# Where a range check's small VectorE sums stand, and how much ScalarE time a planner counts for one matrix unit

## The chip, the cores and the metric

The kernel runs on one core of one Trainium2 chip. The metric is the device time of one execution in microseconds. Every run's time is that of the whole program on the device; a profiled execution also gives its span, from the first to the last instruction.

## The reference, cut to what is computed

One block of a network on 2048 rows of width 512, all in fp32: two modulated layer norms, a Fourier mixing step written as matrix products with cosine and sine tables, and a gated feed-forward step of inner width 1792.

```python
mod = (_silu(c) @ w_mod).reshape(1, 6, 1, -1)
sa, ca, ga, sb, cb, gb = (mod[:, i] for i in range(6))
h = _layernorm(x) * (1 + ca) + sa
a, b = h @ dft_hid_re.T, h @ dft_hid_im.T
x = x + ga * (dft_seq_re @ a - dft_seq_im @ b)
h = _layernorm(x) * (1 + cb) + sb
x = x + gb * ((_silu(h @ w1) * (h @ w3)) @ w2)
```

(The last seven lines stand for the reference's `einsum` calls, with the same operands.)

## The kernel before

**Numbers as pairs.** TensorE multiplies in fp32r. Each fp32 operand is split into a high part (a copy by ScalarE, rounded to fp32r) and a low part (the difference, by VectorE), and a product takes three passes: high by high, high by low, low by high (`PASSES`). So each operand costs one ScalarE and one VectorE instruction, and the copies and differences named `hf`, `h2h`, `w3h`, `w3l`, `w3sh`, `w3sl` are these.

**Stages.** The kernel first makes the modulation and the first layer norm with the hidden transform, then the transform along the sequence, then the second layer norm, and from about 260 us on the feed-forward part. There the inner width is cut into 7 groups of 256 columns (`NG = 7`), and the rows into 4 tiles of 512, which are taken in two pairs: pair 0 are the tiles 0 and 2, pair 1 the tiles 1 and 3. `items` lists the pieces of work in their order: groups 2 to 6 of pair 0, then groups 0 to 6 of pair 1, twelve in all. `turning` is 5, the number of the first item of pair 1.

**Strassen units.** In one item both first products, with `w1` (kind "a") and with `w3` (kind "b"), are 2x2 block products done with seven multiplications each, in a Strassen form. `factor(i, w, n)` does multiplication n: six matmuls of 128x512 into one PSUM bank, then what reads the bank. For n of 1, 5 and 6 ScalarE copies the bank to a tile `x`; for 2, 3 and 7 VectorE adds an earlier copy to the bank; n = 4 is used as it stands. The bank goes on being accumulated into: multiplication 7 adds to the bank that 6 left, so its first matmul has to wait until ScalarE has copied the bank out. Results of "a" pass through a Silu on ScalarE; results of "b" are multiplied by them on VectorE (`times(v, v, src)`), which gives `v`, the operand of the second product.

**Second products.** The five items of `SEVEN` (groups 0 to 4 of pair 1) also do their second product, with `w2`, in seven multiplications. One of them is a unit of `seven_unit` (line 1325): six matmuls into two banks, two read-outs by ScalarE into a tile `y` (line 335, scaled by `gb`), and one DMA, issued by GpSimd, that adds `y` to a sum in DRAM (line 1352). The other items use `down_unit`: one bank and one read-out a unit; for the last two groups of pair 1 VectorE adds the bank straight to the tile `xr` that will be the output (line 1146).

**Order on the engines.** There is no scheduler here that moves instructions: each engine runs its own instructions in the order in which this Python code writes them, and waits on semaphores. The order of the units is a string written by hand, one for each item. The item before the last, number 10, and the last, number 11, have

```python
if i == len(items) - 2:
    body = "a6 y a5 y a7 a3 y a4 b1 y b2 b6 y b5"
if i == len(items) - 1:
    head = "-b7 y a1 a2 y -b4 y -b3 "
    body = "a6 a5 a7 a3 a4 b1 b2 y b6 y b5 y b7 y b4 y y b3 y y y y y y y y y y"
```

where "a6" is multiplication 6 of kind "a" of this item, "-b4" multiplication 4 of kind "b" of the item before, and "y" one unit of second products. So items overlap: the last three multiplications of "b" stand in the head of the next item.

**What is written between the units.** `behind(n, fn)` keeps a step back until n units later (`delayed()` runs at the start of each unit). In items that are not of `SEVEN` the high part of a `v` comes one unit after it and the low part two units after it. The weights for the coming items are loaded, split and summed by steps in the queue `jobs`. After each unit, `beside(us, used)` says how long the unit takes on TensorE (1.36) and how much of that it uses of VectorE and of ScalarE; the rest is credit, and steps of `jobs` are written as long as the credit of their engine is above zero:

```python
for n, us in enumerate((dve, act)):
    credit[n] = min(credit[n] + us, max(us, 1.0))
...
    if any(us > 0 and credit[n] <= 0 for n, us in enumerate(cost)):
        return
```

`USED["y"]` is (0.0, 0.6): a unit "y" is counted as 0.6 us of ScalarE and leaves it a credit of 0.76.

**The check's sums.** Squares of the transform tables are summed by ScalarE into the tile `chk` early in the kernel. `judge()` (line 1009) makes one number of them, `bad`: a memset of the tile `sq` by GpSimd (line 1014), then 15 small VectorE instructions (lines 1015 to 1035). At the program's very end every engine reads `bad` and branches: if it is set, a general version of the whole computation runs, which it does not for these inputs. `judge()` is called in `unit`, right behind multiplication 4 of kind "b" of the item `turning + 1`, which is item 6, so in the head of item 7.

Of the kernel before, what the change touches and what calls it, by code (L numbers as in the profile page):

```python
# [23 lines left out]
NG = F // (2 * P)  # L24
# [18 lines left out]
def folded(nc, pools, c, cp, wmr, wmc, x, xt, ctr, cti, wdr, wdi, w1, w3, w2, out):  # L43
# [73 lines left out]
    def advance(dve, act=9.0, queue=background):  # L117

        for n, us in enumerate((dve, act)):
            credit[n] = min(credit[n] + us, max(us, 1.0))  # L120
        while queue and len(free) >= queue[0][0] + kept():
            _, *cost, fn = queue[0]
            if any(us > 0 and credit[n] <= 0 for n, us in enumerate(cost)):
                return
            queue.popleft()
            if fn is None:
                return
            for n, us in enumerate(cost):
                credit[n] -= us
            fn()  # L130

    def drain(ready, queue=background):
        while not ready():
            fn = queue.popleft()[-1]
            if fn is not None:
                fn()
# [875 lines left out]
    def judge():  # L1012
        sq = consts.tile([P, 3, 32], F32, name="sq")
        nc.gpsimd.memset(sq, 0.0)
        nc.vector.tensor_reduce(
            out=sq[:, 0, :8],
            in_=chk.rearrange("p a b n -> p (a b) n"),
            axis=AX.X,
            op=OP.add,
        )  # L1020
        nc.vector.transpose(sq[:, 1, :], sq[:, 0, :])
        r = small.tile([P, 1], F32, name="jr", tag="jr")
        nc.vector.tensor_reduce(out=r, in_=sq[:, 1, :], axis=AX.X, op=OP.add)
        for a in range(4):
            nc.vector.tensor_copy(sq[:32, 2, a : a + 1], r[32 * a : 32 * a + 32, :])
        nc.vector.tensor_reduce(out=r[:32], in_=sq[:32, 2, :], axis=AX.X, op=OP.add)
        nc.vector.tensor_copy(sq[:32, 0, :], r[:32].to_broadcast([32, 32]))
        nc.vector.transpose(sq[:32, 1, :], sq[:32, 0, :])
        own = small.tile([1, 4], F32, name="own", tag="jo")
        nc.vector.tensor_scalar(own, sq[0:1, 1, 4:8], SMALL, None, op0=OP.mult)  # L1030
        fine = small.tile([1, 4], F32, name="fine", tag="jf")
        nc.vector.tensor_tensor(out=fine, in0=sq[0:1, 1, 0:4], in1=own, op=OP.is_lt)
        times(fine[:, 0:2], fine[:, 0:2], fine[:, 2:4])
        times(fine[:, 0:1], fine[:, 0:1], fine[:, 1:2])
        nc.vector.tensor_scalar(bad, fine[:, 0:1], -1.0, 1.0, op0=OP.mult, op1=OP.add)
# [42 lines left out]
    def delayed():  # L1078
        for fn in later.pop(1, ()):
            fn()  # L1080
        for n in sorted(later):
            later[n - 1] = later.pop(n)


    def up_block(g, t, q, w):
        if q == 0 and w == "w1":
            drain(lambda: ("h2", t, 1) in done)
        to = bank(turn[0] % 4)
        turn[0] += 1
        for d in range(ND):  # L1090
            at = slice(d * P, (d + 1) * P)
            product(
                to,
                [u[:, q, at] for u in wuse[w, g]],
                [u[t, d // 2][:, d % 2, :] for u in (h2h, h2l)],
                d == 0,
                d == ND - 1,
            )
        if t == PAIRS[0][1] and q == 1:
            give_w((w, g))  # L1100
        if w == "w1":
            cur["v"] = take(F32, "v")
            nc.scalar.activation(cur["v"][:, 0, :], to, AF.Silu)
        else:
            v = cur.pop("v")
            times(v[:, 1, :], v[:, 0, :], to)
            u = hf[g, t, q] = take(F32R, "hf")
            copy(u[:, 0, :], v[:, 1, :])
            behind(1, lambda: minus(u[:, 1, :], v[:, 1, :], u[:, 0, :].bitcast(F32)))
            behind(1, lambda: give(v))  # L1110
# [63 lines left out]
    items = [(g, 0) for g in range(2, NG)] + [(g, 1) for g in range(NG)]  # L1174
# [50 lines left out]
    SEVEN = [(g, 1) for g in range(NG - 2)]  # L1225
# [104 lines left out]
    def seven_unit(g, pair, n, key):  # L1330
        new = n in (1, 2, 5)
        if new:
            banks7[:] = [bank(6), bank(7)]
        y = take(F32, "y")
        which, k = TO7[n]
        t = PAIRS[pair][k]
        names = ("h", "l") if LEFT7[n][0] == "h" else ("sh", "sl")
        u = right7.pop(((g, pair), n))
        for e, to in enumerate(banks7):
            at = int(LEFT7[n][1]) * HALF + e * P  # L1340
            product(
                to,
                [flat(wuse[key][x])[:, at : at + P] for x in names],
                [u[:, b, :] for b in range(2)],
                new,
                True,
                not new,
            )
            d = 2 * which + e
            copy_by(y[:, e, :], to, gb[:, d : d + 1])  # L1350
        give(u)
        nc.gpsimd.dma_start(sums[t, which], y, accum_op=OP.add)  # L1352
        behind(4, lambda: give(y))
        if n == ORDER7[-1]:
            for x in wuse.pop(key).values():
                give(x)
            if g == NG - 3:
                for t in PAIRS[pair]:
                    load_sums(t)
# [319 lines left out]

    USED = {"w1": (0.0, 0.5), "w3": (1.2, 0.5), "y": (0.0, 0.6), "own": (0.7, 0.0)}
    FACTOR = {
        "a": {1: (0.0, 0.5), 2: (0.6, 0.5), 3: (0.6, 0.5), 4: (0.0, 0.5), 5: (0.0, 0.5)},
        "b": {1: (0.0, 0.5), 2: (1.8, 0.5), 3: (1.8, 0.5), 4: (1.2, 0.5), 5: (0.0, 0.5)},
# [4 lines left out]
    def beside(us, used):  # L1690
        advance(us - used[0], us - used[1], jobs)
        if not jobs:
            advance(0.0, 0.0)

    def up(g, t):
        for q in range(2):
            for w in ("w1", "w3"):
                drain(lambda: ((w, g), "l") in done, jobs)
                delayed()
                up_block(g, t, q, w)  # L1700
                beside(2.72, USED[w])

    def down(g, pair, *which):
        key = which[-1]
        drain(lambda: (key, "l") in done, jobs)
        delayed()
        if (g, pair) in SEVEN:
            seven_unit(g, pair, *which)
        else:
            down_unit(g, pair, *which)  # L1710
        beside(1.36, USED["own" if pair == 1 and g >= NG - 2 else "y"])

    for w in ("w1", "w3"):
        load_w((w, 1))
# [21 lines left out]
    turning = len([at for at in items if at[1] == 0])  # L1736
# [11 lines left out]
    def early_w3(i):  # L1748
        return items[i][1] == 1

    def unit(kind, i, n):
        g, pair = items[i]
        more = i + 1 < len(items)
        if n == 1:
            drain(lambda: ("ready", i, "w1" if kind == "a" else "w3") in done, jobs)
        if (kind, i, n) == ("a", 0, 6):
            drain(lambda: ("t", 0, 4) in done)
        if (kind, i, n) == ("a", turning, 1):
            drain(lambda: not background)
        if kind == "a" and i == turning and n in (4, 5, 6, 7):  # L1760
            drain(lambda: ("t", 1, {6: 2, 5: 1, 7: 3, 4: 4}[n]) in done, jobs)
        delayed()
        factor(i, "w1" if kind == "a" else "w3", n)
        if (kind, i, n) == ("b", turning + 1, 4):
            judge()
        if (kind, n) == ("a", 1):
            load_w(("w1", *items[i + 1]) if more else ("w2", g, pair))
        if (kind, n) == ("a", 6):
            load_w(("w2", g, pair))
        if not more and kind == "a" and state[i, "w1"]["n"] == 7:  # L1770
            down_banks[:] = [6, 7, 0, 1, 2]
        if (kind, n) == ("a", 7 if i == turning else 3) and more:
            load_w(("w3", *items[i + 1]))
            weight_jobs(i + 1, "w1")
        if (kind, n) == ("b", 2):
            (seven_jobs if (g, pair) in SEVEN else plain_jobs)(("w2", g, pair))
        if (kind, n) == ("b", 3):
            if i + 2 == turning:
                drain(lambda: ("xc", 3) in done)
                for at in ((1, 0), (1, 1), (3, 1)):  # L1780
                    chunk_parts(background, *at, 3)
                sums_of.append(pair_sums(background, 1))
            if i + 1 == turning:
                other_operands()
            if more and not early_w3(i):
                weight_jobs(i + 1, "w3")
            if (g, pair) in SEVEN:
                seconds.extend((g, pair, n, ("w2", g, pair)) for n in ORDER7)
            else:
                for t in PAIRS[pair]:  # L1790
                    seconds.extend((g, pair, t, d, ("w2", g, pair)) for d in range(ND))
        if (kind, n) == ("b", 6) and more and early_w3(i):
            weight_jobs(i + 1, "w3")
        beside(1.36, FACTOR[kind][n])
# [835 lines left out]
```

## Time and profile before

| | before |
|---|---|
| time, median of 3 runs | 700.3 us (699.35 to 700.66) |
| profiled execution, time | 698.81 us |
| its span | 697.0 us, so 1.81 us lie around it |
| TensorE busy | 677.9 us, 97% of the span |
| VectorE busy | 587.9 us, 84% |
| ScalarE busy | 451.4 us, 65% |
| GpSimd busy | 133.6 us, 19% |
| instructions | 9026 |

In the rows of the timeline the first number is the start in us from the span's start, the second the time it takes in us; PE is TensorE, DVE VectorE, ACT ScalarE, POOL GpSimd. "out<-in" names the tiles, "x2" two like instructions in one row, and a bracket at the end the idle time of the engine before the row and what ended it. Successive matmuls of 128x512 start 0.226 us apart when nothing holds them, though each is shown with 0.39 us.

### The profile page before, as it was taken

The page shows a single profiled execution, that of the slowest core. Times are in us where ns is not written, and L with a number is a line of the kernel's source. Part 1 is how long each engine was busy: PE and PEld are TensorE (multiplying, and loading weights), DVE is VectorE, ACT ScalarE, POOL GpSimd, SP SyncE. Part 2 cuts the span into 40 slices and gives each one's busy share as a digit, 9 for nine tenths or more (in the row PEclk, how much of TensorE's full clock was granted, in tenths as well). Part 3 has the DMA queues.
Part 4 walks back from the last instruction along what each step waited for, and adds up shares of the span by engine and source line. Part 5 has one row for each costly group of instructions (what it writes and reads, how often), then busy time and mean ns, then how long its engine had stood idle before and what let it go on. Part 6 is the DMA issues. An engine that isn't in the chain of part 4 may idle for free.

```text
span 697.0 us, 9026 instructions
## 1 busy us (share of the span) xinstructions
PE 677.9 (97%) x3122; PEld 557.1 (80%) x3122; DVE 587.9 (84%) x945; ACT 451.4 (65%) x751; POOL 133.6 (19%) x156
## 2 busy tenths in 40 slices
PE   7999899999999999999999999999999999999996
PEld 5898778888888888888877788787877888888785
DVE  5999779987999977989987886898899979888373
ACT  4998965455343665664566767677676978777620
POOL 1320253543445000100100001011002221121100
PEclk9999999999999999999999999999999999999999
DMA  8730299787578431363758566456939898999703
GB/s 265 217 122 1 74 329 364 254 291 243 186 287 294 152 140 31 63 119 121 133 114 166 132 151 124 88 94 144 265 87 200 150 221 163 187 212 170 186 39 125
DMA packets 40261, 116.80 MB, mean 168 GB/s; under 512 B 5136, under 2 KB 5392, under 8 KB 40208
## 3 DMA queue, kind: packets, MB, share of 16 engines
q0 software_dynamic: 14512, 50.86, 35.8%
q1 hardware_dynamic: 25264, 63.98, 27.6%
q10 hardware_dynamic: 432, 1.31, 0.6%
q8 instruction: 26, 0.43, 0.3%
q14 instruction: 27, 0.22, 0.1%
HBM read 76.81 MB, written 41.42 MB: 170 GB/s over the span
## 4 chain that ended last, share of the span: by engine, by line
PE 73%; DVE 11%; ACT 8%; issue 3%; DMA 3%; SPq 1%; another core or an unknown queue 1%; POOL 0%; ACTq 0%; POOLq 0%
PE bank L100 45%; PE bank L750 25%; PE bank L559 1%; DMA wmr<-in_wmr 1%; ACT y L335 1%; DMA sum<-y 1%; ACT hf L87 1%; DVE v L96 1%; PE bank L598 1%; DVE xc L96 1%; SPq L231 1%; ACT xc L894 1%; DVE x L93 1%; DVE w3s L90 1%; DVE v L93 1%
## 5 line engine op out<-in xcount | busy, mean ns | idle before, releaser
L100 PE MATMUL bank<-hf,w2h 128*128 128x512 f32 (+1 forms) x352 | 108.8, 390 | 0.5 <-ACT y L335 0.4
L87 ACT ACTIVATE hf<-v 128x512 fp32r<-128x512 f32 x71 | 44.3, 630 | 64.6 <-DVE v L96 53.8
L335 ACT ACTIVATE y<-bank,gb 128x512 f32<-128x512 f32 x118 | 76.5, 682 | 5.2 <-PE bank L100 5.1
L100 PEld LDWEIGHTS bank<-hf,w2h 128*128 128x128 f32 x352 | 65.4, 188 | 16.9 <-ACT y L335 2.2
L1160 POOL DMA_DIRECT2D sum<-y x28 | 24.0, 857 | 245.1 <-ACT y L335 125.1
L100 PE MATMUL bank<-hf,w2l 128*128 128x512 f32 (+1 forms) x176 | 68.1, 387 | 0.0
L90 DVE TENSOR_TENSOR hf<-v,hf 128x512 fp32r<-128x512 f32 x71 | 48.8, 687 | 13.8 <-ACT hf L87 13.8
L1352 POOL DMA_DIRECT2D sum<-y x35 | 29.8, 852 | 129.3 <-ACT y L335 124.9
L750 PE MATMUL bank<-d,us 128*128 128x512 f32 x128 | 49.9, 390 | 1.0 <-DVE ho L93 1.0
L750 PE MATMUL bank<-bh,us 128*128 128x512 f32 x128 | 49.9, 390 | 0.0
L750 PE MATMUL bank<-bh,ul 128*128 128x512 f32 x128 | 49.8, 389 | 0.0
L750 PE MATMUL bank<-d,uh 128*128 128x512 f32 x128 | 49.8, 389 | 0.0
L750 PE MATMUL bank<-l,us 128*128 128x512 f32 x128 | 49.8, 389 | 0.0
L750 PE MATMUL bank<-l,uh 128*128 128x512 f32 x128 | 49.8, 389 | 0.0
L170 POOL DMA_INDIRECT re<-in_ctr,mirror x32 | 37.2, 1162 | 65.6 <-DVE ul L90 38.5
L87 ACT ACTIVATE x<-bank 128x512 f32<-128x512 f32 x72 | 41.5, 591 | 11.9 <-PE bank L100 11.8
L170 POOL DMA_INDIRECT im<-in_cti,mirror x32 | 32.8, 1025 | 36.6 <-PE bank L750 11.6
L100 PEld LDWEIGHTS bank<-hf,w2l 128*128 128x128 f32 x176 | 33.0, 188 | 6.7
L93 DVE TENSOR_TENSOR v<-bank,x 128x512 f32<-128x512 f32 x36 | 24.7, 687 | 15.9 <-PE bank L100 14.8
L1244 ACT ACTIVATE v<-v 128x512 f32<-128x512 f32 x36 | 22.7, 630 | 23.2 <-DVE v L93 22.8
L93 DVE TENSOR_TENSOR x<-bank,x 128x512 f32<-128x512 f32 x36 | 24.6, 685 | 9.4 <-PE bank L100 9.1
L100 PE MATMUL bank<-h2h,w1h 128*128 128x512 f32 x80 | 31.1, 389 | 0.0
(260 smaller groups left out, 1906.3 us busy)
## 6 DMA issues: line engine op xcount, KB each, us to landing
sum<-y POOLq DMA_DIRECT2D x63, 512.0 KB
w<-in_w SPq DMA_DIRECT2D x42, 512.0 KB
re<-in_ctr SPq DMA_DIRECT2D x32, 256.0 KB
im<-in_cti SPq DMA_DIRECT2D x32, 256.0 KB
wmc<-in_wmc SPq DMA_DIRECT2D x8, 512.0 KB
xr<-in_xt SPq DMA_DIRECT2D x8, 512.0 KB
sum<-xr SPq DMA_DIRECT2D x8, 512.0 KB
x<-in_x SPq DMA_DIRECT2D x11, 256.0 KB
```

The source lines that it names most:

```text
L87: nc.scalar.activation(dst, src, AF.Copy, scale=scale)
L90: nc.vector.tensor_tensor(out=dst, in0=a, in1=b, op=OP.subtract)
L93: nc.vector.tensor_tensor(out=dst, in0=a, in1=b, op=OP.add)
L96: nc.vector.tensor_tensor(out=dst, in0=a, in1=b, op=OP.mult)
L100: nc.tensor.matmul(acc, lhs[a], rhs[b], start=first and n == 0, stop=last and n == len(PASSES) - 1, skip_group_check=more,)
L170: nc.gpsimd.indirect_dma_start(dst, None, rows, bass.IndirectOffsetOnAxis(ap=at, axis=0))
L231: queue.dma_start(raw_w[dt][q * 64 : (q + 1) * 64, m, :], w[i][par::2, q])
L335: nc.scalar.activation(dst, src, AF.Identity, scale=by)
L750: nc.tensor.matmul(acc[what, e], lhs, rhs, start=begin and i == 0, stop=(end or (turn and what == "x")) and i == len(terms) - 1, skip_grou ...
L1160: nc.gpsimd.dma_start(sums[t, d // 2], y, accum_op=OP.add)
L1244: behind(k != 0 or q == 0, lambda: nc.scalar.activation(v, src, AF.Silu))
L1352: nc.gpsimd.dma_start(sums[t, which], y, accum_op=OP.add)
```

## The change

Two edits. In the table `USED` a unit of second products in a `SEVEN` item is now counted with 1.3 us of ScalarE, both its read-outs, where it was counted with 0.6. And `judge()` is written behind multiplication 4 of "b" of item `len(items) - 2`, which is item 10 (the last group but one of pair 1), in the head of the last item, where it was written behind that of item 6.

```diff
-    USED = {"w1": (0.0, 0.5), "w3": (1.2, 0.5), "y": (0.0, 0.6), "own": (0.7, 0.0)}
+    USED = {"w1": (0.0, 0.5), "w3": (1.2, 0.5), "y": (0.0, 0.6), "y7": (0.0, 1.3), "own": (0.7, 0.0)}
...
             down_unit(g, pair, *which)
-        beside(1.36, USED["own" if pair == 1 and g >= NG - 2 else "y"])
+        wide = (g, pair) in SEVEN
+        beside(1.36, USED["own" if pair == 1 and g >= NG - 2 else "y7" if wide else "y"])
...
         factor(i, "w1" if kind == "a" else "w3", n)
-        if (kind, i, n) == ("b", turning + 1, 4):
+        if (kind, i, n) == ("b", len(items) - 2, 4):
             judge()
```

TensorE's and SyncE's order stay as they were, instruction for instruction. On ScalarE five pairs of neighbours change places, one in each of the items 6 to 10, and nothing else. In items 6 to 9 it is the high part of the next `w3` (`w3h`) and the copy of bank 5 after multiplication 5 of "b" (`x`): `w3h` stood first and now stands second. In item 10 it is the high part of the sums of `w3` (`w3sh`) and the same copy `x`. ScalarE's rows there, before:

```order
L335 ACTIVATE y_5833<-bank_952_5831,gb 128x512
L335 ACTIVATE y_5833<-bank_953_5832,gb 128x512
L87 ACTIVATE w3sh_5845<-w3s_5825 128x1024
L87 ACTIVATE x_5854<-bank_957_5847 128x512
L87 ACTIVATE hf_5866<-v_5622 128x512
```

And ScalarE's rows of the changed kernel at the same place:

```order
L335 ACTIVATE y_5813<-bank_952_5811,gb 128x512
L335 ACTIVATE y_5813<-bank_953_5812,gb 128x512
L87 ACTIVATE x_5832<-bank_956_5825 128x512
L87 ACTIVATE w3sh_5834<-w3s_5805 128x1024
L87 ACTIVATE hf_5846<-v_5602 128x512
```

What moved is `w3sh`, behind one bank copy; the high part `hf` behind both keeps its place.

On VectorE the 15 instructions of `judge()` leave the head of item 7 and stand in the head of item 11. There VectorE's rows were, before, from the product of multiplication 4 (`v` with `bank`) on:

```order
L96 TENSOR_TENSOR v_5622<-v_5622,bank_943_5782 128x512
L90 TENSOR_TENSOR hf_5918<-v_5622,hf_5918 128x512
L93 TENSOR_TENSOR x_5789<-bank_957_5847,x_5789 128x512
L96 TENSOR_TENSOR v_5621<-v_5621,x_5789 128x512
L90 TENSOR_TENSOR hf_5947<-v_5621,hf_5947 128x512
```

In the changed kernel VectorE has, from inside the sums on (six of their rows, beginning with the tile `sq`, stand between that product and these):

```order
L1028 STREAM_TRANSPOSE sq<-sq 32x32
L1030 TENSOR_SCALAR own<-sq 1x4
L1032 TENSOR_TENSOR fine<-sq,own 1x4
L96 TENSOR_TENSOR fine<-fine 1x2
L96 TENSOR_TENSOR fine<-fine 1x1
L1035 TENSOR_SCALAR bad<-fine 1x1
L90 TENSOR_TENSOR hf_5918<-v_5602,hf_5918 128x512
L93 TENSOR_TENSOR x_5769<-bank_956_5825,x_5769 128x512
L96 TENSOR_TENSOR v_5601<-v_5601,x_5769 128x512
L90 TENSOR_TENSOR hf_5947<-v_5601,hf_5947 128x512
```

The sums now stand ahead of the low part `hf_5918`, of the addition `x` from the bank of multiplication 3, and of the product `v` made from it.

On GpSimd the memset of `sq` goes along. Its last rows, before:

```order
L1352 DMA sum_0_3248<-y_5833 128x1024
L1352 DMA sum_0_3779<-y_5868 128x1024
L1352 DMA sum_1_3781<-y_5901 128x1024
L1352 DMA sum_1_3250<-y_5920 128x1024
L2566 TENSOR_LOAD bad
```

And those of the changed kernel:

```order
L1352 DMA sum_0_3248<-y_5813 128x1024
L1352 DMA sum_0_3779<-y_5848 128x1024
L1352 DMA sum_1_3781<-y_5881 128x1024
L1014 MEMSET sq 128x96
L1352 DMA sum_1_3250<-y_5920 128x1024
L2567 TENSOR_LOAD bad
```

The memset now stands behind the last DMA but one of the second products, where at its old place (behind the DMA of another unit) it is gone.

## The prediction, as it was put on record

> **What bounds the kernel now.** I read the page first, then who TensorE waited for, then the timeline of each engine around the two places of the sums and the five swapped pairs.
>
> The page of the kernel before, its head and the busy times:
>
> ```profile
> span 697.0 us, 9026 instructions
> PE 677.9 (97%) x3122; PEld 557.1 (80%) x3122; DVE 587.9 (84%) x945; ACT 451.4 (65%) x751; POOL 133.6 (19%) x156
> ```
>
> TensorE is busy for 97% of the span, and its order does not change. So the time moves only where TensorE's next matmul starts later or earlier than now. TensorE's waits from 450 to 560 us, which is where the old place of the sums lies:
>
> ```profile
> PE bank L100 <- ACT y L335: 1.0, 2, 0.6
> PE bank L100 <- DVE v L93: 0.3, 1, 0.3
> PE bank L100 <- ACT x L87: 0.2, 1, 0.2
> ```
>
> From 560 us to the end the same view lists no wait. That is not quite so: a matmul is drawn with 0.39 us while the next one starts 0.226 us after it, so a wait shorter than the difference stays hidden. I therefore go by the distances between starts.
>
> **The old place of the sums: what goes.** The timeline of the kernel before, VectorE's and GpSimd's rows, then ScalarE's (the third is from the next item, where no sums stand), then TensorE's:
>
> ```profile
> 532.08 0.68 DVE L96 TENSOR_TENSOR v<-v,bank 128x512 f32<-128x512 f32 x1
> 532.42 0.85 POOL L1352 DMA_DIRECT2D sum<-y  x1 [3.89 <-ACT y L335]
> 532.96 0.51 POOL L1014 MEMSET sq<- 128x96 f32 x1
> 533.50 0.42 DVE L1015 TENSOR_REDUCE sq<-chk 128x8 f32<-128x256 f32 x1 [0.75 <-POOL sq L1014]
> ...
> 536.52 0.67 DVE L90 TENSOR_TENSOR hf<-v,hf 128x512 fp32r<-128x512 f32 x1
> 537.12 0.67 DVE L93 TENSOR_TENSOR x<-bank,x 128x512 f32<-128x512 f32 x1
> ```
>
> ```profile
> 539.28 0.63 ACT L87 ACTIVATE hf<-v 128x512 fp32r<-128x512 f32 x1 [2.57 <-DVE v L90]
> 539.82 1.25 ACT L335 ACTIVATE y<-bank,gb 128x512 f32<-128x512 f32 x2
> ...
> 566.25 0.64 ACT L87 ACTIVATE hf<-v 128x512 fp32r<-128x512 f32 x1 [0.22 <-DVE v L90]
> ```
>
> ```profile
> 539.76 0.39 PE L100 MATMUL bank<-th,w1sl 128*128 128x512 f32 x1
> 540.54 0.72 PE L100 MATMUL bank<-hf,w2h 128*128 128x512 f32 x2 [0.39 <-ACT y L335]
> ```
>
> The sums wait for the memset, which starts 0.54 us after the DMA issue ahead of it (532.42 to 532.96); the first sum starts 0.54 us after that. From the first sum to the low part behind them VectorE needs 3.02 us (533.50 to 536.52). All of it delays the `v` for which ScalarE's `hf` waits 2.57 us; the read-out `y` stands behind that `hf`, and TensorE needs the bank that `y` empties. Its start comes 0.78 us after the one before, 0.55 too late, and its first pair takes 0.72 where a pair takes 0.61: 0.66 us together. One item later, without sums, the same `hf` waits 0.22 us and TensorE not at all. **Gain here: 0.66 us**, at least 0 if another wait steps in at once, at most this.
>
> **The swaps in items 6 to 9: nothing.** ScalarE's rows in the last of the four, then the VectorE row that reads `w3h`:
>
> ```profile
> 610.88 1.06 ACT L87 ACTIVATE w3h<-w 128x1024 fp32r<-128x1024 f32 x1
> 611.83 0.60 ACT L87 ACTIVATE x<-bank 128x512 f32<-128x512 f32 x1
> 612.31 1.28 ACT L335 ACTIVATE y<-bank,gb 128x512 f32<-128x512 f32 x2
> ```
>
> ```profile
> 613.47 1.22 DVE L90 TENSOR_TENSOR w3l<-w,w3h 128x1024 fp32r<-128x1024 f32 x1
> ```
>
> A copy takes 0.48 us of ScalarE's row (611.83 to 612.31). Put first, it starts at 610.88, and `w3h` runs from 611.36 to 612.42; the read-out behind both stays at 612.31. `w3l` comes at 613.47, 1.05 us after that, behind other VectorE work. The copy of bank 5 comes 0.95 us earlier, but what reads it stands behind `w3l` too. The cover is that 1.05 us of VectorE's backlog; were it gone, 0.48 us would be lost an item.
>
> **The swap in item 10: 0.46 us lost.** Here the pair is `w3sh` and the copy. TensorE's last matmul of multiplication 5, then ScalarE, VectorE, and TensorE's next wait:
>
> ```profile
> 639.80 0.39 PE L100 MATMUL bank<-th,w3sl 128*128 128x512 f32 x1
> ...
> 645.24 0.39 PE L100 MATMUL bank<-h2h,w1l 128*128 128x512 f32 x1
> 645.73 0.73 PE L100 MATMUL bank<-hf,w2sh 128*128 128x512 f32 x2
> ```
>
> ```profile
> 640.77 1.07 ACT L87 ACTIVATE w3sh<-w3s 128x1024 fp32r<-128x1024 f32 x1
> 641.72 0.60 ACT L87 ACTIVATE x<-bank 128x512 f32<-128x512 f32 x1
> 644.47 0.63 ACT L87 ACTIVATE hf<-v 128x512 fp32r<-128x512 f32 x1 [2.15 <-DVE v L96]
> 645.01 1.25 ACT L335 ACTIVATE y<-bank,gb 128x512 f32<-128x512 f32 x2
> ```
>
> ```profile
> 641.89 1.22 DVE L90 TENSOR_TENSOR w3sl<-w3s,w3sh 128x1024 fp32r<-128x1024 f32 x1
> ```
>
> The bank is ready at 640.19, so the copy starts at 640.77 without a wait and `w3sh` runs from 641.25 to 642.32. VectorE's `w3sl`, which started 0.05 us after `w3sh` ended, starts at 642.35 and not at 641.89: 0.46 later. VectorE has no slack behind it: the addition and the `v` follow at once, ScalarE's `hf` waits 2.15 us for that `v`, `y` stands behind `hf`, and TensorE's start at 645.73, already 0.26 late, waits for `y`. So all of it is 0.46 us later from here on. Bounds: 0, if VectorE had slack that the rows do not show, and 0.48, the whole copy.
>
> **The new place of the sums: 2.33 us more.** VectorE and GpSimd, ScalarE, and TensorE in the head of item 11:
>
> ```profile
> 648.80 0.69 DVE L96 TENSOR_TENSOR v<-v,bank 128x512 f32<-128x512 f32 x1 [1.33 <-PE bank L100]
> 649.58 0.85 POOL L1352 DMA_DIRECT2D sum<-y  x1 [2.18 <-ACT y L335]
> ...
> 651.81 0.69 DVE L93 TENSOR_TENSOR x<-bank,x 128x512 f32<-128x512 f32 x1 [0.94 <-PE bank L100]
> 652.54 0.69 DVE L96 TENSOR_TENSOR v<-v,x 128x512 f32<-128x512 f32 x1
> ```
>
> ```profile
> 653.40 0.63 ACT L87 ACTIVATE hf<-v 128x512 fp32r<-128x512 f32 x1 [2.10 <-DMA sum<-y]
> 653.94 1.19 ACT L87 ACTIVATE x<-bank 128x512 f32<-128x512 f32 x2
> ```
>
> ```profile
> 654.11 0.39 PE L100 MATMUL bank<-th,w1sl 128*128 128x512 f32 x1
> 654.57 0.50 PE L100 MATMUL bank<-th,w1sh 128*128 128x512 f32 x1
> ```
>
> Unlike at the old place, item 10 is not of `SEVEN`: the high part `hf` of the `v` from multiplication 3 is due one unit later and so stands ahead of ScalarE's copy of bank 0 after multiplication 6, and multiplication 7 (654.57) cannot start before that copy. The sums stand ahead of that `v` on VectorE. Step by step, with the 0.46 us:
>
> - The DMA issue comes at 649.58 + 0.46 = 650.04, the memset 0.54 later at 650.58, the first sum 0.54 later at 651.12. VectorE, free at 649.95, has waited 1.17 us.
> - The low part behind the sums: 651.12 + 3.02 = 654.14. The addition 0.60 later (536.52 to 537.12): 654.74. The `v` 0.73 later (651.81 to 652.54): 655.47, done after 0.69 at 656.16.
> - ScalarE's `hf` at 656.19; the DMA that it waited for now (653.40) has landed long before. The copy 0.54 later (653.40 to 653.94): 656.73. TensorE 0.63 after the copy's start (653.94 to 654.57): 657.36.
>
> That is 2.79 us later than 654.57, of which 0.46 is the swap. TensorE stands still for 2.56 us there (it would be ready at 654.11 + 0.23 + 0.46). Behind it the matmuls already stand end to end, so nothing gives the time back. Bounds for the sums here: below, as if they began as soon as VectorE is free (651.12 - 1.15), which takes 1.15 off; above, 2.79 alone with no gain elsewhere.
>
> What is queued behind the sums on VectorE has been named; behind the waiting `hf` on ScalarE stand both copies, for multiplications 7 and 3. GpSimd has one DMA behind the memset, and no one waits for it before VectorE's first addition to the output tiles, in the first "y" of the last item's body, seven multiplications on.
>
> **A stall that long and TensorE's clock.** The start of the trace has one of like length; TensorE's row and the stretch behind it (the value behind the busy times of the five engines is the granted clock):
>
> ```profile
> 9.00 1.10 PE L485 MATMUL bank<-ident,x 128*128 128x128 f32 x4 [2.08 <-DVE x L470]
> ...
> 10.00:15.00 5.00, 5.00 (x29) 3.87 (x28) 4.26 (x7) 2.69 (x5) 0.00 (x0) 0.76 1.08 274
> ```
>
> After 2.08 us of idleness five microseconds went at 0.76 of the clock, 1.2 us of work lost. If the new stall did the same, the loss would be 2.79 + 1.2. The row is from a TensorE that had just begun, and I take nothing for it, but keep it as a rival. The Trainium skill, "TensorE: Matmul & The Clock Gate", section "HAM oscillation — how this bites in real kernels", says that only idle gaps of more than about 3.4 us bring the half clock back; by it the sum has no such term, as the stall is an estimated 0.8 us short of that. No run here has yet shown a gap of this length in a warm TensorE.
>
> **The sum.** -0.66 + 0.46 + 2.33 = +2.13 us. The profiled execution took 698.81 us, 697.0 of span and 1.81 around it; with the change 700.94. That execution lies 1.49 us under the median of the runs, 700.3; on the median's footing the changed kernel takes 702.4 us, 0.3% longer.
>
> **Rivals.**
>
> 1. *VectorE's idle time in the last item takes the sums in.* VectorE waits 1.33 and 0.94 us for TensorE around the new place, so little work might seem free there. Then only the old stall goes: 700.3 - 0.66 = 699.6. Against it: TensorE loses nothing only if the copy starts by 654.17, so the sums would have to begin by 648.56, before the product ahead of them is even made (648.80). Chance 0.06. If the swaps freed TensorE from all 1.5 us that the waits from 450 to 560 list, it would be 698.8, faster than before; but the waits for `y` and `x` there stand on instructions that are not moved. Chance 0.03.
> 2. *The memset runs at once.* If GpSimd did not hold it behind the DMA issue, or the issue came early, the sums would begin at 649.97: +2.13 - 1.15 = +0.98, 701.3. Against it stands the old place, where VectorE waited 0.75 us for that memset. Chance 0.10.
> 3. *The old stall does not go.* If another ScalarE wait holds `y` at 540 us, the gain is lost: 700.3 + 2.79 = 703.1. For it: ScalarE is full there. Against it: the next items have the same order and no wait. Chance 0.09.
> 4. *The stall costs clock as well:* 702.4 + 1.2 = 703.6. Chance 0.06.
>
> **How the numbers follow.** My forecast has 0.66, with the swap in item 10 between 0 and 0.48, so 702.0 to 702.4 before the scatter of the runs (1.3 us from lowest to highest). About 0.2%, 1.4 us, is what a measurement of this kernel can tell from no change, so the line lies at 701.7. Rivals 3 and 4 and nearly all of the forecast lie above it, 0.77; rivals 1 and 2 mostly below, with a rest of the forecast, 0.19; faster 0.04. The range goes from 701.1, which takes in rival 2, to 703.6, rival 4.
>
> **What would show it.** In the changed kernel's trace: no late start of TensorE near 540 us; `w3l` of items 6 to 9 with no wait for `w3h`; `w3sl` near 642 about 0.46 us later against TensorE; the sums starting about 0.54 us after the memset, 3.0 us long, in the head of item 11; and one start of TensorE some 2.8 us after the one before it, with ScalarE's copy `x` behind an `hf` that waited for VectorE's `v`. I am wrong if TensorE goes through multiplication 7 of the last item without that gap, or if it gains more than 0.7 us before 640 us.

## The result and the profile after

Six runs of the changed kernel have a median of 705.22 us (704.39 to 707.65), six of the kernel before, measured beside it, 699.83 (698.79 to 700.66). Slower, by 5.4 us between the medians. The ratio on record, which is not that of the medians, is 1.0084, with a 95% interval of 1.0070 to 1.0099. The prediction had 702.4 with a range up to 703.6. Its side was right, its size was not.

The profiled execution of the changed kernel took 705.42 us, 6.61 more than that of before. The head of its page:

```profile
span 703.6 us, 9020 instructions
...
PE 679.8 (97%) x3122; PEld 558.9 (79%) x3122; DVE 588.2 (84%) x945; ACT 451.9 (64%) x751; POOL 132.5 (19%) x156
```

TensorE has the same 3122 matmuls, and is busy 1.9 us longer with them (677.9 before). The whole program has 9020 instructions and not 9026, although the change takes no work away: by the records of the traces, VectorE has five waiting instructions fewer and SyncE one (352 records before, 351 after). Both are traces of what the prediction lacked. First what it had, in the order of its steps. TensorE's timeline at the old place, then ScalarE's in item 9 and VectorE's row behind it:

```profile
540.50 0.39 PE L100 MATMUL bank<-th,w1sl 128*128 128x512 f32 x1
540.73 0.61 PE L100 MATMUL bank<-hf,w2h 128*128 128x512 f32 x2
```

```profile
610.39 1.08 ACT L87 ACTIVATE x<-bank 128x512 f32<-128x512 f32 x2
611.35 1.07 ACT L87 ACTIVATE w3h<-w 128x1024 fp32r<-128x1024 f32 x1
612.30 1.27 ACT L335 ACTIVATE y<-bank,gb 128x512 f32<-128x512 f32 x2
```

```profile
613.45 1.22 DVE L90 TENSOR_TENSOR w3l<-w,w3h 128x1024 fp32r<-128x1024 f32 x1
```

The second unit at 540 starts 0.23 us after the matmul ahead of it, not 0.78. In item 9 the copy is first, the read-out `y` comes at 612.30 (612.31 before), and `w3l` has no wait. Now item 10 and the new place: ScalarE, VectorE, GpSimd, TensorE.

```profile
640.76 0.60 ACT L87 ACTIVATE x<-bank 128x512 f32<-128x512 f32 x1
641.23 1.08 ACT L87 ACTIVATE w3sh<-w3s 128x1024 fp32r<-128x1024 f32 x1
...
656.28 0.63 ACT L87 ACTIVATE hf<-v 128x512 fp32r<-128x512 f32 x1 [4.53 <-DVE v L96]
656.81 0.58 ACT L87 ACTIVATE x<-bank 128x512 f32<-128x512 f32 x1
```

```profile
642.34 1.22 DVE L90 TENSOR_TENSOR w3sl<-w3s,w3sh 128x1024 fp32r<-128x1024 f32 x1 [0.38 <-ACT w3sh L87]
...
651.11 0.42 DVE L1015 TENSOR_REDUCE sq<-chk 128x8 f32<-128x256 f32 x1 [1.19 <-POOL sq L1014]
...
654.18 0.69 DVE L90 TENSOR_TENSOR hf<-v,hf 128x512 fp32r<-128x512 f32 x1
...
655.50 0.69 DVE L96 TENSOR_TENSOR v<-v,x 128x512 f32<-128x512 f32 x1
```

```profile
650.04 0.85 POOL L1352 DMA_DIRECT2D sum<-y  x1 [2.17 <-ACT y L335]
650.58 0.51 POOL L1014 MEMSET sq<- 128x96 f32 x1
```

```profile
645.23 0.39 PE L100 MATMUL bank<-h2h,w1l 128*128 128x512 f32 x1
646.19 0.73 PE L100 MATMUL bank<-hf,w2sh 128*128 128x512 f32 x2 [0.57 <-ACT y L335]
...
654.59 0.39 PE L100 MATMUL bank<-th,w1sl 128*128 128x512 f32 x1
657.45 0.80 PE L100 MATMUL bank<-th,w1sh 128*128 128x512 f32 x1 [2.47 <-ACT x L87]
658.04 0.63 PE L100 MATMUL bank<-tl,w1sh 128*128 128x512 f32 x1
658.47 0.63 PE L100 MATMUL bank<-th,w1sl 128*128 128x512 f32 x1
```

Up to 657.45 this is the prediction's list: the sums at 651.11 (it had 651.12), the low part 654.18 (654.14), `v` 655.50 (655.47), the copy 656.81 (656.73), TensorE 657.45 (657.36). The last two rows are new: matmuls 0.43 us apart, where all before stand 0.23 apart. The windows around them (sum of the stretch, the five engines' busy times, then the granted clock):

```profile
653.62:657.03 3.41, 1.35 (x6) 0.77 (x5) 2.53 (x8) 0.75 (x2) 0.00 (x0) 1.00 1.05 198
657.03:660.45 3.42, 3.00 (x7) 2.42 (x8) 0.60 (x1) 0.85 (x2) 0.00 (x0) 0.50 0.39 67
660.45:663.86 3.41, 3.41 (x16) 2.81 (x16) 1.38 (x2) 1.86 (x3) 0.00 (x0) 1.00 1.01 400
```

TensorE runs at half its clock for 3.41 us, from 657.03 on, before the wait is over. And the end. VectorE's last addition, before and then after, and SyncE's waits in the last block of its program, before and then after (us in total, times, longest). Below each stand the packets of the instruction queue q14 from SyncE's branch into that block to the end of the span (packets, MB, share):

```profile
690.38 0.48 DVE L1146 SCALAR_TENSOR_TENSOR xr<-bank,gb,xr 128x256 f32<-128x256 f32 x1 [0.23 <-PE bank L100]
```

```profile
694.60 0.48 DVE L1146 SCALAR_TENSOR_TENSOR xr<-bank,gb,xr 128x256 f32<-128x256 f32 x1 [0.23 <-PE bank L100]
```

```profile
SPq L2572 <- SPq L2572: 2.6, 1, 2.6
...
q14 instruction: 4, 0.03, 2.0%
```

```profile
SPq L2573 <- SPq L2573: 5.0, 2, 2.7
...
q14 instruction: 5, 0.04, 1.8%
```

The last addition comes 4.22 us later, but the span ends 6.6 later. From the end of that addition to the end of the span, which I call the tail, it is 697.0 - 690.86 = 6.1 us before and 703.6 - 695.08 = 8.5 after. In it SyncE waits for 0.7 us for TensorE's sequencer, in both, and else for itself alone: once for 2.6 us before, and twice, for 5.0 us, after. The second of the two lies between the first and the second of the block's eight waiting instructions (699.1 to 701.4 us), and from the branch to the end one packet of code more, of 8 KB, is moved; the profile doesn't say for which engine.

So the account of this pair of profiles: 0 up to 645.23 (at 540 this execution was 0.74 us behind that of before, 540.50 against 539.76 for the same matmul, most of it from the first 100 us, and the gain there brought the two level); 657.45 - 654.57 = 2.88 from the swap and the sums; 4.22 - 2.88 = 1.34 from the half clock; 2.4 from the tail: 6.6 us, of 6.61 measured.

### The profile page after: what moved, and what is told of

It is laid out like the page before. It is cut to its first block, busy times and chain, and to the rows that moved or that the text cites. A ratio compares the mean times of both kernels' runs of the same rounds, so it can differ in the third digit from the quotient of the medians.

```text
span 703.6 us, 9020 instructions
## 1 busy us (share of the span) xinstructions
PE 679.8 (97%) x3122; PEld 558.9 (79%) x3122; DVE 588.2 (84%) x945; ACT 451.9 (64%) x751; POOL 132.5 (19%) x156
## 4 chain that ended last, share of the span: by engine, by line
PE 75%; DVE 11%; ACT 9%; issue 3%; DMA 1%; another core or an unknown queue 0%; POOL 0%; SPq 0%; ACTq 0%
PE bank L100 46%; PE bank L750 25%; PE bank L559 2%; ACT y L335 1%; ACT hf L87 1%; DVE v L96 1%; PE bank L598 1%; DVE x L93 1%; DMA x<-in_x 1%; DVE w3sl L90 1%; DVE xc L96 1%; ACT hm L501 1%; DVE v L93 1%; ACT xc L894 1%; DVE st L449 1%
## 5 line engine op out<-in xcount | busy, mean ns | idle before, releaser
L170 POOL DMA_INDIRECT re<-in_ctr,mirror x32 | 35.4, 1105 | 65.6 <-DVE ul L90 39.0
L100 PE MATMUL bank<-th,w1sh 128*128 128x512 f32 x72 | 28.9, 401 | 3.4 <-ACT x L87 3.4
```

The lines of the kernel that those rows point to most:

```text
L100: nc.tensor.matmul(acc, lhs[a], rhs[b], start=first and n == 0, stop=last and n == len(PASSES) - 1, skip_group_check=more,)
L170: nc.gpsimd.indirect_dma_start(dst, None, rows, bass.IndirectOffsetOnAxis(ap=at, axis=0))
```

## The experiments

Theory A, on the tail: SyncE's program is one instruction shorter. Its transfers keep their order, but not its waits: the transfer `xr<-sum` at L1115 waits for three semaphores, not four, and the separate waiting instruction for the fourth is gone. (So the sentence ahead of the prediction, that SyncE's order stays instruction for instruction, holds for the transfers alone. The runs below show that the constant brings this about; that it does so by handing out the tiles in another order is likely and not shown.) SyncE's last block, which holds the eight waits of the end, begins, counted in the program's list, at its instruction 591 instead of 592, and if code is loaded in pieces with a border there, the block lies in two pieces. Its rival B: the tail belongs to the sums' new place or to the late end. Theory C, on the clock: the wait itself takes TensorE to half its clock. Its rival D: chance, or the chip's load.

**The sums alone.** ScalarE's constant is 0.6 again:

```
-    ... "y7": (0.0, 1.3), ...
+    ... "y7": (0.0, 0.6), ...
```

> Of the change only the sums move; ScalarE's time of a second unit stays 0.6, so no w3sh waits behind a copy x. All theories: no late TensorE start at 540, the sums begin 0.46 us earlier than in the changed kernel, TensorE's wait for a7's copy x stays about 2.5 us, the last VectorE addition of xr moves up by about 0.46 us against the changed kernel. They differ in the tail, from the end of that last addition to the end of the span (6.14 us before, 8.52 changed). Theory A (SyncE's program is one instruction shorter in the changed kernel, through the new constant, and its last eight waits then come behind one more code load): SyncE has its old count here, so the tail is 6.1 us and the time is 705.2 - 0.5 - 2.4 = 702.3 us, 1.0035 of before. Theory B (the sums' new place lengthens the tail): tail 8.5 us, 704.7 us. In both, if a half-clock stretch of 3.4 us follows the wait, the matmuls behind it start 0.43 us apart.

**The constant alone.** The sums at their old place:

```
-        if (kind, i, n) == ("b", len(items) - 2, 4):
+        if (kind, i, n) == ("b", turning + 1, 4):
             judge()
```

> Of the change only the constant: ScalarE's time of a second unit with three operands 1.3, the sums at their old place. All theories: the late TensorE start near 540 is back (0.66 us), the copy w3sh waits behind x as in the changed kernel, TensorE's start behind y +0.46 us near 646, no wait of 2.5 us at 657 and no half clock there. Theory A (the constant makes SyncE's program one instruction shorter, and its last waits come behind one more code load): tail from the last addition to the end 8.5 us, time 699.8 + 0.5 + 2.4 = 702.7 us. Theory B (the tail belongs to the sums' new place or to the late end itself): tail 6.1 us, time 700.3 us.

**One more instruction on SyncE.** The changed kernel, and ahead of its first transfer:

```
+    nc.sync.drain()
     nc.sync.dma_start(cc, cp)
```

> The changed kernel with one SyncE drain ahead of its first transfer, so that its program has as many SyncE instructions as before. Theory A (code load at the end): the tail falls from 8.5 to 6.1 us, nothing else moves, 705.2 - 2.4 = 702.8 us. Theory B (the tail has another cause): tail stays 8.5 us, 705.2 us.

Measured, as ratios to before on the same chip: sums alone 1.0030 (1.0013 to 1.0046), constant alone 1.0036 (1.0023 to 1.0049), the drain 1.0034 (1.0018 to 1.0051). Theory A had 1.0035, 1.0041 and 1.0043; B's 1.0070 for the first, 1.0007 for the second and the unmoved 1.0077 for the third lie outside. SyncE's waits in its last block, for the three in turn:

```profile
SPq L2573 <- SPq L2573: 2.6, 1, 2.6
```

```profile
SPq L2573 <- SPq L2573: 5.0, 2, 2.6
```

```profile
SPq L2575 <- SPq L2575: 2.7, 1, 2.7
```

The tail goes with SyncE's count, not with the place of the sums or the hour of the end. B falls. Nor is it VectorE's count: the drain leaves VectorE its five instructions fewer, and the tail is short.

**Matmuls in the wait.** The changed kernel, with 10 matmuls whose result no one reads, ahead of the last item's multiplication 7:

```
+        if (kind, i, n) == ("a", len(items) - 1, 7):
+            spare = bank(7)
+            for _ in range(10):
+                nc.tensor.matmul(spare, flat(wuse["w1", g, pair]["h"])[:, :P],
+                    right(pair, 7)[0][:, 0, :], start=True, stop=True)
         factor(i, "w1" if kind == "a" else "w3", n)
```

> The changed kernel with 10 matmuls of 512 columns into a bank that nothing reads, on TensorE just ahead of the last item's a7, so that TensorE is busy for about 2.1 of the 2.5 us in which it waits for the copy x. Theory C (the wait takes TensorE to half its clock for one stretch of 3.4 us, which costs 1.3 us): a7 starts as late as in the changed kernel (657.4), but the granted clock stays 1.00 behind it, matmuls start 0.22 us apart, the last addition comes 1.3 us earlier and the time is 705.2 - 1.3 = 703.9 us. Theory D (the half clock is a matter of the chip's load or of chance, not of the wait): the clock falls as before, 705.2 us. The tail is 8.5 us in both.

TensorE's timeline and the granted clock behind it:

```profile
654.44 2.43 PE L1767 MATMUL bank<-th,w1h 128*128 128x512 f32 x10
657.10 0.50 PE L100 MATMUL bank<-th,w1sh 128*128 128x512 f32 x1 [0.23 <-ACT x L87]
```

```profile
657.50:660.00 2.50, 2.50 (x13) 2.02 (x12) 0.69 (x1) 0.44 (x2) 0.00 (x0) 1.00 0.16 26
```

The clock stays, as C has it, and the ratio 1.0055 (1.0030 to 1.0080) is C's 1.0058; but D's 1.0077 is within the interval. One of the 8 executions has a mean clock of 0.990 and the longest span (703.4 us, the others 699.7 to 702.0); without a trace of it, where it lost clock is open. And the runs with the sums alone and with the drain kept their clock in the profile too, with a wait of the same 2.5 us. TensorE's rows, and the windows, of the drain:

```profile
656.30 0.50 PE L100 MATMUL bank<-th,w1sh 128*128 128x512 f32 x1 [2.49 <-ACT x L87]
```

```profile
654.49:657.90 3.41, 1.59 (x7) 1.33 (x8) 1.26 (x2) 1.60 (x3) 0.00 (x0) 1.00 0.79 157
657.90:661.31 3.41, 3.41 (x17) 2.83 (x16) 1.38 (x2) 1.86 (x3) 0.00 (x0) 1.00 0.41 132
```

So neither C nor D as I had put them. In every trace each drop and rise of the clock lies a whole number of 3.413 us from the others: in the profile after, the drops at 73.35, 657.03 and 698.0 and the rises at 76.8 and 660.45. The clock is thus judged in windows that run on by themselves, and where they fall on the wait differs from execution to execution. I laid this grid over the traces and added up in each window the time in which columns went through TensorE: 0.227 us for each matmul of 512, the distance of starts at full clock, and less for narrower ones. At the wait, and at a slack place near 70 us, these windows had the least:

| window from (us) | streaming in 3.41 us | clock in the next window |
|---|---|---|
| after 653.62 / 69.94 | 1.19 / 1.33 | half / half |
| constant alone 69.39 | 1.27 | half |
| memset early (below) 69.39 | 1.29 | half |
| one unexecuted (below) 655.72 / 68.63 | 1.38 / 1.27 | half / half |
| 127 unexecuted (below) 68.39 | 1.39 | half |
| sums alone 651.67 | 1.46 | full |
| one more on SyncE 654.49 | 1.46 | full |
| changed again (below) 650.83 | 1.87 | full |
| before 70.47 | 1.93 | full |

At 1.39 us (41%) and less the next window was at half clock, at 1.46 (43%) and more it was not. In the traces not listed the emptiest window at these places had 1.6 us or more, and the clock stayed. Theory E, then: the wait costs the clock in those executions in which enough of it falls into one window.

**The changed kernel again, and both mended.** The second has the drain and the 10 matmuls. They, and the next two, share one chip.

> The changed kernel once more, on the same chip as the three runs beside it. What the runs so far make of it: +2.1 us by the sum of the prediction's terms, +2.4 us for the second code load of SyncE's last block, and 0 or +1.35 us for a half-clock stretch, by where the chip's clock windows of 3.41 us happen to fall on the wait of 2.5 us: 4.5 to 5.9 us over before, the runs in two groups 1.3 us apart.

> The changed kernel with the SyncE drain of one run and the 10 matmuls in the wait of another, together. If the prediction's terms were right and the code load and the clock are all that it left out, the time is before + 2.1 us (ratio 1.003), the tail is 6.1 us, and no half-clock stretch follows the wait in any execution. If something else is missing, it stays over 3 us above before.

The changed kernel: 702.12 us, ratio 1.0062 (1.0040 to 1.0084), and its runs are not in two clear groups (spans 699.5 to 703.6), so that part of the expectation was too neat. Both mended: 700.04 us, ratio 1.0026 (1.0015 to 1.0036), against 698.11 of before, +1.9 us where the prediction's sum has +2.13. None of its 12 runs has a mean clock below 0.995; of the 12 with the drain alone, whose tail is as short, four have 0.991 to 0.993, and they are the four longest (spans 700.1 to 701.9 against 697.7 to 699.3). That is in line with Theory E and no proof of it: the two ran on different chips, and the kernel before, which has no such wait, has a mean clock of 0.993 or less in 5 of 31 executions on the drain's chip and in 1 of 26 on the other. On the same chip as both mended, the changed kernel has such a clock in 2 of 6. The wait that the prediction forecast is still there, filled:

```profile
656.15 0.50 PE L100 MATMUL bank<-th,w1sh 128*128 128x512 f32 x1 [0.24 <-ACT x L87]
```

```profile
SPq L2585 <- SPq L2585: 2.6, 1, 2.6
```

**The memset early.** In the changed kernel the memset of `sq` is taken out of `judge` and issued behind multiplication 1 of `w3` in the same item (`ready()` makes the tile and does the memset):

```
+        if (kind, i, n) == ("b", len(items) - 2, 1):
+            ready()
```

> The changed kernel with the memset of sq put into GpSimd's queue three units earlier (behind b1 of the last item but one), so that the sums find it done. The terms of the prediction: sums start where v ends, about 1.15 us earlier, TensorE waits 1.3 us for the copy x instead of 2.5. Clock by windows (a window of 3.41 us with TensorE busy in under about 40% of it halves the next one): a wait of 1.3 us leaves at least 1.9 us busy (55%) in any window, so no half clock in any execution; the tail of 8.5 us stays. Time: changed - 1.15 us in executions that kept the clock, - 2.5 us against those that lost it: before + 3.4 us. If any wait costs the clock: before + 4.8 us.

VectorE's and TensorE's timelines:

```profile
648.07 0.69 DVE L96 TENSOR_TENSOR v<-v,bank 128x512 f32<-128x512 f32 x1 [1.31 <-PE bank L100]
648.67 0.41 DVE L1020 TENSOR_REDUCE sq<-chk 128x8 f32<-128x256 f32 x1
```

```profile
654.99 0.50 PE L100 MATMUL bank<-th,w1sh 128*128 128x512 f32 x1 [1.20 <-ACT x L87]
```

The sums follow `v` at once and TensorE waits 1.20 us instead of 2.47. The emptiest window there has 1.92 us of streaming, and the clock stays. Ratio 1.0045 (1.0031 to 1.0059), 3.1 us over before: what Theory E has with the long tail (3.4), not the 4.8 of a clock lost at any wait. That no execution loses clock is not borne out: two of the nine have a mean of 0.988 and 0.991 and the longest spans (701.4 and 701.0 us, the others 698.6 to 699.8), and where they lost it no trace shows.

**The sums in VectorE's idle stretch.** Behind multiplication 4 of `w1` in the last item, ScalarE's constant 0.6:

```
-        if (kind, i, n) == ("b", len(items) - 2, 4):
+        if (kind, i, n) == ("a", len(items) - 1, 4):
             judge()
```

> The sums behind a4 of the last item, where VectorE waits 3.46 us for TensorE in the trace of before (658.4 to 661.8), the memset long done, ScalarE's constant back at 0.6. If the sums' cost is only where they stand in VectorE's queue: the late start at 540 goes (-0.66 us), the sums of 3.0 us end before the next x is wanted, no wait of TensorE at 657, SyncE's count and the tail (6.1 us) as before: before - 0.66 us (ratio 0.9991). If the sums cost something wherever they stand (their copies, their use by the branch at the end): before + 0 to + 2 us.

```profile
655.25 0.69 DVE L93 TENSOR_TENSOR v<-bank,x 128x512 f32<-128x512 f32 x1 [0.60 <-PE bank L100]
655.86 0.41 DVE L1015 TENSOR_REDUCE sq<-chk 128x8 f32<-128x256 f32 x1
...
658.81 0.14 DVE L1035 TENSOR_SCALAR bad<-fine 1x1 int32<-1x1 f32 x1
659.40 0.69 DVE L93 TENSOR_TENSOR x<-bank,x 128x512 f32<-128x512 f32 x1 [0.45 <-PE bank L100]
```

VectorE still waits 0.45 us for TensorE behind the sums, so they cost nothing there. 697.36 us against 698.11, 0.75 us less, ratio 0.9991 (0.9981 to 1.0001): in line with the 0.66 us of the old stall, though the interval just reaches no change. It is 0.7% under the changed kernel on the same chip.

**How large the pieces of code are.** The kernel before, with 15 and with 7 drains ahead of SyncE's first transfer, and with 127 in the general branch, which is not executed; and the changed kernel with one drain in that branch. Each was run once, 0.3 us above, 0.4 below, 2.2 above and 3.8 above a single execution of before; single times scatter by more than 1 us, so what counts here are the traces:

```
 def general(nc, pools, ...):
     consts, small, big, psum = pools
+    for _ in range(127):
+        nc.sync.drain()
```

> The kernel before with 15 drains on SyncE ahead of its first transfer; its last block, with the eight waits, then begins at SyncE's instruction 607 instead of 592 (changed kernel: 591). Theory A1 (code comes in pieces of 16 instructions: 592 = 37 x 16, so 591 and 607 are the last of a piece and the waits behind them need a second one): SyncE waits twice in its last block, about 5.0 us instead of 2.6, the tail behind the last addition is 8.5 us instead of 6.1, and the span is 2.4 us longer. Theory A2 (what counts is the length alone, and any program at least as long as before ends as fast): one wait of 2.6 us, tail 6.1 us.

> The kernel before with 7 drains on SyncE ahead of its first transfer; its last block begins at SyncE's instruction 599. Theory A1 with pieces of 16 instructions: the waits lie in the piece from 592 to 607, one wait of 2.6 us, tail 6.1 us, time as before. Pieces of 8 instructions: 599 is the last of a piece, two waits, about 5.0 us, tail 8.5 us.

> The kernel before with 127 drains on SyncE in the general branch, which is not executed; its last block begins at instruction 719 = 591 + 128, and nothing that is executed changes. The run with 15 more (607) showed that pieces of 16 are wrong. Theory A3 (code comes in larger pieces, 128 instructions or a fraction of it above 16: the profile's instruction queue of SyncE, q14, moves 0.22 MB in 27 packets, some 8 KB each): 719 lies in its piece as 591 does, SyncE waits twice, about 5.0 us, tail 8.5 us, span 2.4 us longer. Theory A2 (a program at least as long as before ends as fast): one wait, 2.6 us, tail 6.1 us.

> The changed kernel with one SyncE drain in the general branch, which is not executed: the last block begins at 592 as before, and no executed instruction differs from the changed kernel. Theory A: one wait of 2.6 us in SyncE's last block and a tail of 6.1 us. If the drain that was executed at the start had its effect by its own time or by the transfers behind it: two waits, 8.5 us.

SyncE's waits in its last block, in this order, and for the first and the third q14's packets from SyncE's branch to the end:

```profile
SPq L2574 <- SPq L2574: 2.6, 1, 2.6
...
q14 instruction: 4, 0.03, 2.4%
```

```profile
SPq L2574 <- SPq L2574: 2.6, 1, 2.6
```

```profile
SPq L2574 <- SPq L2574: 5.0, 2, 2.8
...
q14 instruction: 5, 0.04, 1.9%
```

```profile
SPq L2575 <- SPq L2575: 2.6, 1, 2.6
```

Pieces of 16 (A1) are wrong. One instruction that is never executed makes the changed kernel's tail short, and 127 of them make that of before long: A3. The border at 592 comes again 128 instructions on (in one run), not 16. In the run with 15 more the 25 records of the block, 607 to 631 by the program's count, would cross a border of pieces of 32 at 624, and no second wait is there; so pieces of 64 or 128 fit, unless SyncE had fetched the next one ahead. In all six traces with a second wait it lies behind the first instruction of the block. The total of q14's packets, which the third expectation calls SyncE's, decides nothing: it is 28 in the run with 15 more too, whose tail is short. All kernels by the start of SyncE's last block:

| last block begins at | kernels | tail, us | SyncE's waits in it, us |
|---|---|---|---|
| 592 | before, sums alone, one more, both mended, idle stretch, one unexecuted | 5.9 to 6.3 | 2.6 to 2.8 |
| 599, 607 | seven more, fifteen more | 6.1, 5.9 | 2.6 |
| 591 | after, again, constant alone, matmuls in the wait, memset early | 8.0 to 8.6 | 4.9 to 5.0 |
| 719 | 127 unexecuted | 8.2 | 5.0 |

## Why the prediction was right and wrong

- *The old place, -0.66*: right. No late start near 540, and the run with the sums in the idle stretch has 0.75 us less than before, with an interval that just reaches zero.
- *The swaps in items 6 to 9, nothing*: right, by the cover that was named.
- *The swap in item 10, +0.46*: right. `w3sl` starts 0.45 later and TensorE 0.46 (645.73 to 646.19).
- *The sums at the new place, +2.33*: right; with the swap 2.88 measured, 2.79 forecast, and each step of the chain within 0.1 us. Its lower bound, a memset that is done early, took 1.27 us off TensorE's wait (2.47 to 1.20) where 1.15 was given.
- *"I take nothing for it"*, of the clock: wrong. The like row from the start of the trace had shown it, at 1.2 us; it was set aside since TensorE had just begun there, and the rival got 0.06. (The stretch read there, 10 to 15 us, also left out the first microsecond of the half clock, which began at 9.03.) From multiplication 7 to the last addition TensorE needed 35.8 us in executions that kept the clock, 37.2 in the profile after, 37.4 in one other. What the wait costs is thus 0, or 1.3 to 1.6 us. Of the wait's 2.63 us without a column, 2.0 must fall into one window (3.41 less about 1.4); sliding the window over it, that is so in about six phases of ten, an estimate from those two numbers (of the five profiles with this wait unfilled, two lost the clock). The term to put in was some 0.8 us, with both ends kept.
- The Trainium skill, "TensorE: Matmul & The Clock Gate", is right here in "Part 1: The HAM clock gate (the "warmup" mystery)", that the window is 3413 ns long and runs freely. Its limit of about 3.4 us of idleness, in "HAM oscillation — how this bites in real kernels", is not: 2.47 us were enough.
- *The sum carried to the end*: wrong, and the step that failed most. It took everything behind TensorE's last matmul over from before. No term and no rival looked at SyncE's program, and so the 2.4 us of a second code load were missed, the largest piece of the error. The order of SyncE's instructions shows that it has one less. A row of before has the price of one load, SyncE's wait of 2.6 us on itself; that the block began exactly at a border, no row of before could have told.
- The Trainium skill, "Runtime: NRT & Kernel Launch", section "Instruction fetch mechanics", says that code comes in blocks of 256 instructions, that crossing a border is mostly hidden, and that a taken branch to code that is not loaded stalls for the fetch. In these runs the border comes again after 128. The wait of 2.6 to 2.8 us behind the branch agrees with the last of the three; the border just behind it was not hidden either, and cost 2.4 us.

Together: 2.13 + 2.4 + a share of 1.34 is 4.5 to 5.9; the two measurements of the changed kernel are 5.4 and 4.0 us over before, from medians of six runs. The second lies 0.5 under that span, but inside its own interval, which is 2.8 to 5.9 us. With the load and the wait mended 1.9 are left (1.0 to 2.5), so nothing else of the size of these two terms is missing.

## What to carry to other kernels

A stall of TensorE that is shorter than a clock window can still cost more than itself: count how many of the 3.41 us would be left busy, and add what a half clock costs (here 1.3 to 1.6 us) times the share of phases in which it is too little. Look beyond the last matmul as well: where engines end in a block of their own behind a branch, an instruction more or less anywhere ahead of it can move that block across a border of code. Small work goes where its engine already waits, and first its own helpers, such as the memset here, have to be done.

## What the runs showed of the hardware

- The granted clock is judged in windows of 3.413 us that run on whatever the program does (before: a drop at 9.03 and one at 695.11, 201 windows apart). At the two places of the table 1.39 us of streaming or less in a window gave half the clock in the next one, 1.46 or more did not.
- This goes with part of the spread between executions of one kernel: of 31 executions of before on one chip the five with a mean clock of 0.993 or less have spans of 698.1 to 700.6 us, the others 695.4 to 698.1. With the same order of TensorE up to there the half-clock window came near 9 us in the profile of before, near 73 in that of after, and in that of both mended before the end not at all.
- A code load that SyncE could not hide took 2.6 to 2.8 us behind the branch and 2.2 to 2.4 at the border behind it, and whether that border is met depends also on instructions that are never executed.
